# More products with the identity in the stops of TensorE, and the last rows stored by halves, in a gated linear attention with a squared-ReLU layer

## The chip, the core and the metric

The kernel runs on one NeuronCore of a Trainium2 chip. The metric is the time of one execution on the device, in microseconds; smaller is better. The core has five engines that run side by side, each with its own queue of instructions: TensorE (PE, with PEld for its weight loads), VectorE (DVE), ScalarE (ACT), GpSimd (POOL) and SyncE (SP, which here only issues transfers). They wait for one another through semaphores.

## The reference

Two stages follow each other. The first is a linear attention with a complex decay at each position, for 4 batches of 8 heads, 768 positions and 48 features; the second a layer with 2048 hidden features on the 3072 rows of 384 that come out.

```python
mag = np.sqrt(a_re * a_re + a_im * a_im)
scale = np.minimum(mag, 0.999) / (mag + 1e-06)
a_re_n, a_im_n = (a_re * scale, a_im * scale)
for t in range(S):
    ar, ai = (a_re_n[:, :, t, :, None], a_im_n[:, :, t, :, None])
    new_re = ar * S_re - ai * S_im
    new_im = ar * S_im + ai * S_re
    kv = np.einsum('bhd,bhe->bhde', k[:, :, t], v[:, :, t])
    S_re, S_im = (new_re + kv, new_im)
    y[:, :, t] = np.einsum('bhd,bhde->bhe', q[:, :, t], S_re)
...
h = x @ w_in
r = np.maximum(h, 0.0)
g = r * r
return (g @ w_out).astype(np.float32)
```

## The kernel before

The 3072 rows are cut into six units of 512 positions (`NU` = 6, `L` = 512). For each unit three things are done.

- The chain (`chain`): VectorE and ScalarE normalise the decays and multiply them up over the positions. On its way it needs four sets of three transposes on TensorE (`turned`, L1039): two of the totals (`totals`, with the matrix `perm`) and two back (`back`, with the identity). ScalarE copies their results (L1054 for the totals into `e`, L1220 for the way back into `xn`), and VectorE goes on from there. In the end it multiplies the decays into q and k (`apply`, L1259 to L1273, tile `f`).
- The pairs of heads (`pairs`): queries and keys are turned (for the first units on TensorE, L1375, copied by ScalarE into `QT` at L1379), scores are formed (L1393, tile `sc`) and masked by VectorE (L1396, tile `A`), states are summed (L1421 from the tile `KC`, which transfers bring by L1314; VectorE adds them at L1430 and L1432), and the output of the pair is made in the bank `yp` (L1445, L1449), copied by ScalarE (L1455) and carried by transfers into `xT` (L1463).
- The dense layer (`dense`), twice for each unit, 256 rows at a time (`grp`): 96 matmuls with the first weights (L1485), ReLU and square on ScalarE, and the second weights. For the first unit this is done directly (L1531). Later units use a scheme with seven products of half size in place of eight (`seven`; `half` is the product at L1582, `put`, `copy` and `add` at L1597, L1601 and L1606 are the sums around it). It fills two tiles `ot` of 128 rows by 384 columns: `o0` and `o1`. `rows` stores such a tile when it is complete, by GpSimd's queue, and for the last half of the last unit by SP's. A tile is written by halves of 192 columns, and its key in the planner is `("ot", o, c)` with the half c.

While the first unit's chain runs, the weights are read and converted on VectorE and ScalarE (`convert`, L823 to L836) as well, so VectorE has much to do before the first dense layer.

All of this is written down as steps for a planner (`Plan`). A step has an engine, an estimated duration, what it reads and writes, and a rank. `Plan.order` plays the steps through with these estimates, picks on each engine the lowest rank among those that are ready, and so fixes the order in which the instructions are emitted. The estimates matter for the order alone: on the chip the engines wait for semaphores.

In the same pass the planner looks at TensorE's stops: the time by the plan between the end of its last step and the start of the next (`stop`). Where a stop is longer than `FILL` and one of the banks d0, d1, d2 is free, it puts products of the identity with itself into that bank (L729), which nobody reads. `EACH` is the time that it reckons for one. They are emitted ahead of the step that ends the stop, so they stand in TensorE's queue before it. Each is a matmul of 128 by 128 by 128 in float32, which the trace shows as two records.

At the end VectorE has written a flag that tells whether the values allow this path; every engine loads it, branches around the general path (L1749), and the program ends when all transfers have landed (SP waits for them).

Of the kernel before, what the change touches and what calls it, by code (L numbers as in the profile page):

```python
# [480 lines left out]
class Plan:  # L481
# [4 lines left out]
    SLACK = 2.0  # L486
    RATE = 280e3
    STOP, COLD = 2.5, 3.4
    FILL, EACH = 0.8, 0.22

    def __init__(self, idle, banks):
        self.idle = idle
# [38 lines left out]
    def order(self):  # L531
        steps = self.steps
        users = [[] for _ in steps]
        left = []
        for n, s in enumerate(steps):
            left.append(len(s[2]))
            for d in s[2]:
                users[d].append(n)
        engines = {s[0] for s in steps}
        free = {e: 0.0 for e in engines}  # L540
        wait = {e: [] for e in engines}
        done, start, at = {}, {}, {}
        bus, warm = 0.0, 6.0
        self.fill = {}

        def ready(n):
            e = steps[n][0]
            t = 0.0
            for d in steps[n][2]:
                same = steps[d][0] == e and steps[d][5] is None  # L550
                hop = 0.0 if same else self.HOP[steps[d][0]]
                if e == "PE" and not same and done[d] > 100.0:
                    paired = steps[d][5] is not None and steps[n][6]
                    hop += self.SLACK if paired else self.MARGIN
                t = max(t, done[d] + hop)
            at[n] = t
            wait[e].append(n)

        for n in range(len(steps)):
            if not left[n]:  # L560
                ready(n)
        for _ in steps:
            best = None
            for e in engines:
                if not wait[e]:
                    continue
                t = max(free[e], min(at[n] for n in wait[e]))
                if best is None or t < best[0]:
                    best = (t, e)
            t, e = best  # L570
            n = min((n for n in wait[e] if at[n] <= t), key=lambda n: (steps[n][4], n))
            wait[e].remove(n)
            _, dur, _, _, _, wire, _ = steps[n]
            start[n] = t
            if e == "PE":

                stop = t - free[e]
                spare = [b for b in self.lives if self.spare(b, done, free[e])]
                if spare and stop > self.FILL:
                    self.fill[n] = int((stop - 0.3) / self.EACH), spare[0]  # L580
                elif stop > self.STOP:
                    warm = t + self.COLD
                if t < warm:
                    dur += min(dur, 0.5 * (warm - t))
            free[e] = t + dur
            if wire is None:
                done[n] = t + dur
            else:
                lat, size = wire
                bus = max(bus, t + dur) + size / self.RATE  # L590
                done[n] = max(bus, t + dur) + lat
            for m in users[n]:
                left[m] -= 1
                if not left[m]:
                    ready(m)
        self.start, self.done = start, done
        return sorted(start, key=lambda n: (start[n], n))
# [18 lines left out]
def fast_path(ctx, tc, q, k, v, a_re, a_im, moe_w_in, moe_w_out, out, flag):  # L616
# [6 lines left out]
    C = 128  # L623
    W = 4
    L = W * C
    NU = B * S // L
# [17 lines left out]
    dve, pool, act, sp = nc.vector, nc.gpsimd, nc.scalar, nc.sync  # L644
# [6 lines left out]
    def sb(name, n, dtype=F32, rows=C):  # L651
        return const.tile([rows, n], dtype, name=name)
# [8 lines left out]
    DH = DM // 2  # L661
# [20 lines left out]
    ots = [sb(f"ot{s}", DM) for s in range(NO)]  # L682
# [9 lines left out]
                                                           r=2, b=2)  # L692
# [8 lines left out]
            for n in ("d0", "d1", "d2", "sc0", "sc1", "tr0", "tr1", "yp")}  # L701
# [8 lines left out]
                     in_=turn_.rearrange("p (k x w) -> p k x w", w=4, x=4))  # L710
    pool.memset(mask, 1.0)
    for c in range(W):
        rows = mask[32 * c:32 * c + 32]
        pool.affine_select(out=rows.rearrange("p (c t) -> p c t", c=W),
                           in_=rows.rearrange("p (c t) -> p c t", c=W),
# [4 lines left out]
    for t in txs:  # L720
# [9 lines left out]
                                    stop=True), ["d2", "d1", "d0"])  # L730
# [4 lines left out]
    def tt(n):  # L735
        return n / 960.0 + 0.07
# [9 lines left out]
    def step(*args, **kw):  # L746
        return plan.add(*args, **kw)
# [4 lines left out]
    def dma(q, reads, writes, fn, rank, size, lat=1.8, group=None):  # L752
        name, dur = ("POOL", 0.55) if q is pool else ("SP" if q is sp else "ACT", 0.6)
        step(name, dur, reads, writes, fn, rank, (lat, size), group)

    CHAIN, PAIR, DENSE, CONV, LATE = 2, 1, 3, 3, 5
# [566 lines left out]
    def take(kind, n):  # L1323
        s = slot[kind]
        slot[kind] = s + 1
        if kind == "d":
            plan.lives["d%d" % (s % n)].append([])
        return s % n
# [208 lines left out]
                out=ots[o], in_=ps), (0, n))  # L1537
            rows(n, grp, i, o)

    def rows(n, grp, i, o):  # L1540
        r = n * L + (2 * grp + i) * C
        queue = sp if n == NU - 1 and grp == 1 else pool
        dma(queue, [("ot", o, 0), ("ot", o, 1)], [], lambda: queue.dma_start(  # L1543
            out=out[r:r + C, :], in_=ots[o]), (DENSE, n), C * DM * 4)

# [10 lines left out]
    def parts_of(h, up):  # L1556
        return [("w2", NT // FP * up + 2 * h + i) for i in range(2)]
# [20 lines left out]
    def half(n, b, r, h, w, wkeys, first=True, last=True):  # L1578

        def go():  # L1580
            for j in range(4 * h, 4 * h + 4):
                pe.matmul(bank[b][:, 0:DH], lhsT=g4[:, r, j], rhs=w(j),  # L1582
                          start=first and j == 0, stop=last and j == NT - 1)
        step("PE", 1.32, gk(r, h) + wkeys, [(b,)], go, (DENSE, n))

    def w_lo(c):
        return lambda j: w2[:, j, ts(c, DH)]

    def w_up(c):
        return lambda j: w2[:, NT + j, ts(c, DH)]  # L1590

    def w_t(r):
        return lambda j: TW[:, r, j]

    def put(n, o, x0, x1, op, h):
        sl = slice(4 * h, 4 * h + 4)
        step("DVE", tt(4 * C), gk(x0, h) + gk(x1, h), gk(o, h), lambda: dve.tensor_tensor(  # L1597
            out=g4[:, o, sl], in0=g4[:, x0, sl], in1=g4[:, x1, sl], op=op), (0, n))

    def copy(n, o, c, b):  # L1600
        step("ACT", ac(DH), [(b,)], [("ot", o, c)], lambda: act.copy(  # L1601
            out=ots[o][:, ts(c, DH)], in_=bank[b][:, 0:DH]), (0, n))

    def add(n, o, c, c0, b, o0=None):
        o0 = o if o0 is None else o0
        step("DVE", tt(DH) + 0.01, [("ot", o0, c0), (b,)], [("ot", o, c)], lambda: dve.tensor_tensor(  # L1606
            out=ots[o][:, ts(c, DH)], in0=ots[o0][:, ts(c0, DH)], in1=bank[b][:, 0:DH],
            op=ALU.add), (0, n))
# [19 lines left out]
    def seven(n, grp):  # L1628
        b0, b1, b2 = ["d%d" % take("d", 3) for _ in range(3)]
        o0, o1 = take("ot", NO), take("ot", NO)  # L1630
        g00, g10, g01, g11 = range(4)
        for h in range(2):
            half(n, b0, g00, h, w_lo(0), parts_of(h, 0))
            half(n, b1, g01, h, w_up(0), parts_of(h, 1))
            put(n, g10, g10, g11, ALU.add, h)
            put(n, g00, g10, g00, ALU.subtract, h)
            put(n, g01, g01, g00, ALU.subtract, h)
        copy(n, o1, 1, b0)
        add(n, o0, 0, 1, b1, o1)
        for h in range(2):  # L1640
            half(n, b2, g00, h, w_t(1), [("T", 1, h)])
            put(n, g00, g11, g00, ALU.subtract, h)
        for h in range(2):
            half(n, b0, g10, h, w_lo(1), parts_of(h, 0))
        add(n, o0, 1, 1, b2, o1)
        for h in range(2):
            half(n, b1, g00, h, w_t(0), [("T", 0, h)])
        for h in range(2):
            half(n, b2, g01, h, w_up(1), parts_of(h, 1))
        add(n, o1, 0, 1, b1, o0)  # L1650
        add(n, o1, 1, 0, b0)
        add(n, o0, 1, 1, b0)
        for h in range(2):
            half(n, b1, g11, h, w_t(2), [("T", 2, h)])
        add(n, o0, 1, 1, b2)
        rows(n, grp, 0, o0)
        add(n, o1, 0, 0, b1)
        rows(n, grp, 1, o1)

    def verdict():  # L1660
# [120 lines left out]
```

## Time and profile before

| | us |
|---|---|
| three timed executions | 703.12, 705.86, 706.57 |
| their median | 705.86 |
| the profiled execution, as the device timed it | 707.76 |
| its span, from the first to the last instruction | 705.9 |
| idle products (L729), 520 records, TensorE busy with them | 61.1 |
| L1485, first weights, 1056 records | 236.3 |
| L1582, second weights by halves, 1152 records | 199.6 |
| row stores (L1543), GpSimd and SP | 22 and 2 |

A profile is of one execution, and its times count from the start of the span. Busy time is not time on the path: idle products are busy time of TensorE, though nothing waits for what they write. A row of the order of time gives the start, the duration, the engine, the line, what is written and read, and in brackets how long the engine stood idle before it and what ended that. The mean duration of a matmul record (281 ns for an idle product) overlaps with the next; two starts tell the cost of one. The idle products stand in five places: 284 records from 1.52 us, 118 from 36.05, 8 from 49.56, 106 from 51.29 and 4 from 96.50.

### The profile page before, as it was taken

Reading aid. Unit: us, or ns where it says so; the run is one execution under the profiler, and the core shown is the slowest. Engines: PE = TensorE matmul, PEld = TensorE weight load, DVE = VectorE, ACT = ScalarE, POOL = GpSimd, SP = SyncE. Lnnn points to the kernel's source line nnn. Section 1 sums busy time; section 2 is a strip of 40 time slices with the busy share of each in tenths; the row PEclk is TensorE's granted clock in tenths of the full one; section 3 lists DMA queues with packets and bytes.
Section 4 is the critical chain, followed back from the end, with each engine's and each line's share of the span. In section 5 each row is a group of like instructions: output and inputs, shape, how many; then the busy total and the mean of one; then the engine's idle time right before and its main releaser. Section 6 shows DMA issues by size and latency. Waiting matters only on the chain.

```text
span 705.9 us, 12514 instructions
## 1 busy us (share of the span) xinstructions
PE 685.8 (97%) x4562; PEld 622.3 (88%) x4562; DVE 571.9 (81%) x1173; ACT 348.2 (49%) x578; POOL 175.7 (25%) x334
## 2 busy tenths in 40 slices
PE   9998989999999999999999999999999999999995
PEld 9998878767778999998999998988989989989995
DVE  5989899999888789997998598997699998337631
ACT  6693469955575434377424557233657242132230
POOL 6502553052400004205044050033230033032100
PEclk9999899999999999999999999999999999999998
DMA  9741459130630004735037570036550035288600
GB/s 280 218 175 27 107 134 303 60 67 22 184 88 23 1 23 119 201 86 136 11 103 189 116 154 12 1 101 178 130 153 1 24 89 132 65 294 271 202 3 26
DMA packets 56359, 79.58 MB, mean 113 GB/s; under 512 B 10944, under 2 KB 38464, under 8 KB 56288
## 3 DMA queue, kind: packets, MB, share of 16 engines
q0 software_dynamic: 15232, 40.72, 19.1%
q1 hardware_dynamic: 36928, 32.98, 18.4%
q10 hardware_dynamic: 4128, 4.98, 2.7%
q8 instruction: 38, 0.62, 0.4%
q14 instruction: 33, 0.27, 0.1%
HBM read 48.76 MB, written 4.72 MB: 76 GB/s over the span
## 4 chain that ended last, share of the span: by engine, by line
PE 66%; DVE 22%; DMA 3%; issue 3%; ACT 3%; SPq 1%; POOL 0%; DVEq 0%; ACTq 0%
PE d L1485 26%; PE d L1582 22%; PE sc L1393 4%; PE d L1531 3%; DVE f L1273 3%; DVE f L1259 2%; PE yp L1445 2%; PE tr L1421 2%; PE yp L1449 2%; DMA aq<-in_a_im_dram 2%; PE tr L1485 1%; DVE aq L1263 1%; PE sc L1485 1%; DVE f L985 1%; DVE aq L970 1%
## 5 line engine op out<-in xcount | busy, mean ns | idle before, releaser
L1485 PE MATMUL d<-xT,w 128*128 128x256 f32 x1056 | 236.3, 380 | 2.9 <-issue 2.4
L1485 PEld LDWEIGHTS d<-xT,w 128*128 128x128 f32 x1056 | 198.6, 190 | 31.9 <-issue 3.3
L1582 PE MATMUL d<-w,g 128*128 128x192 f32 x768 | 132.8, 327 | 0.1
L1582 PEld LDWEIGHTS d<-w,g 128*128 128x128 f32 x768 | 124.9, 190 | 1.7 <-issue 0.9
L1516 ACT ACTIVATE g<-d 128x512 f32<-128x512 f32 x88 | 52.1, 592 | 120.2 <-PE d L1485 87.4
L1314 POOL DMA_DIRECT2D KC<-f x160 | 78.4, 498 | 111.7 <-issue 56.4
L1543 POOL DMA_DIRECT2D out_dram<-ot x22 | 12.6, 572 | 242.2 <-DVE ot L1606 117.7
L1582 PE MATMUL d<-T,g 128*128 128x192 f32 x384 | 66.8, 327 | 0.7 <-DVE g L1597 0.7
L1582 PEld LDWEIGHTS d<-T,g 128*128 128x128 f32 x384 | 62.8, 190 | 1.4 <-DVE g L1597 1.2
L729 PE MATMUL d<-ident 128*128 128x128 f32 x520 | 61.1, 281 | 1.5 <-POOL ident masks.py:199 1.5
L903 POOL DMA_DIRECT2D v<-in_v_dram x80 | 46.4, 587 | 65.0 <-issue 32.7
L1597 DVE TENSOR_TENSOR g<-g 128x512 f32<-128x512 f32 x64 | 43.1, 684 | 23.5 <-ACT g L1517 16.4
L1517 ACT ACTIVATE g<-g 128x512 f32<-128x512 f32 x96 | 60.6, 631 | 3.0
L729 PEld LDWEIGHTS d<-ident 128*128 128x128 f32 x520 | 60.5, 197 | 1.5 <-POOL ident masks.py:199 1.5
L1393 PE MATMUL sc<-QT 96*128 96x128 f32 x368 | 48.1, 285 | 1.2 <-ACT QT L1379 1.2
L1455 ACT COPY yt<-yp 112x512 f32<-112x512 f32 x24 | 26.2, 1091 | 45.0 <-PE yp L1449 45.0
L1393 PEld LDWEIGHTS sc<-QT 96*128 96x128 f32 x368 | 45.0, 198 | 3.2 <-ACT QT L1379 1.6
L1259 DVE TENSOR_TENSOR f<-aq,xn 128x384 f32<-128x384 f32 (+1 forms) x64 | 45.1, 750 | 2.0 <-ACT xn L1220 1.9
L1273 DVE TENSOR_TENSOR f<-aq 128x384 f32<-128x384 f32 (+1 forms) x64 | 44.9, 753 | 0.6
L1531 PE MATMUL d<-w,g 128*128 128x384 f32 x128 | 44.3, 488 | 0.0
L1396 DVE TENSOR_TENSOR A<-sc,mask 128x512 f32<-128x512 f32 x45 | 29.7, 681 | 15.9 <-PE sc L1393 15.8
L985 DVE TENSOR_TENSOR f<-aq 128x384 f32<-128x384 f32 x72 | 36.9, 554 | 0.9
(195 smaller groups left out, 993.0 us busy)
## 6 DMA issues: line engine op xcount, KB each, us to landing
QT<-aq SPq DMA_DIRECT2D x128, 64.0 KB, 2.2
f<-in_moe_w_in_dram POOLq DMA_DIRECT2D x8, 768.0 KB, 7.1
f<-in_moe_w_out_dram POOLq DMA_DIRECT2D x8, 768.0 KB, 6.2
KC<-f POOLq DMA_DIRECT2D x104, 48.0 KB, 2.6
out_dram<-ot POOLq DMA_DIRECT2D x22, 192.0 KB, 2.5
QT<-aq ACTq DMA_DIRECT2D x64, 64.0 KB, 2.5
v<-in_v_dram POOLq DMA_DIRECT2D x80, 48.0 KB, 2.9
xT<-yt SPq DMA_DIRECT2D x36, 96.0 KB, 2.4
```

What stands on the lines that cost most here:

```text
L729: plan = Plan(lambda b: pe.matmul(bank[b][:, 0:C], lhsT=ident, rhs=ident, start=True, stop=True), ["d2", "d1", "d0"])
L903: lambda i=i, c=c, src=src: pool.dma_start(out=t[32 * c:32 * c + 32, i], in_=src[c]), vrank, 32 * 1536, 4.0,
L985: dve.tensor_tensor(out=f, in0=a[:, :, :, c - 1], in1=a[:, j, :, c].unsqueeze(1).to_broadcast([C, 2, HH, D]), op=ALU.mult)
L1259: lambda j=j, r=r: dve.tensor_tensor(out=f4[:, j, r], in0=a[:, r], in1=over(j), op=ALU.mult), late[z])
L1273: lambda j=j, r=r, o=o: dve.tensor_tensor(out=o[:, :, :, r * D:(r + 1) * D], in0=qk[:, j], in1=a[:, r], op=ALU.mult), late[z])
L1314: lambda i=i, c=c, queue=queue: queue.dma_start(out=kc[32 * c:32 * c + 32, i], in_=nat[32 * i:32 * i + 32, c]),
L1393: pe.matmul(sa[:, j], lhsT=T[:, j, 1, h], rhs=T[:, j, 0, h], start=True, stop=True)
L1485: pe.matmul(ps, lhsT=w1[:, f // FP, m, ts(f % FP, C)], rhs=xT[:, n % 2, m, ts(grp, G)], start=(m == 0), stop=(m == NM - 1))
L1516: act.activation(out=o, in_=ps, func=AF.Relu)
L1517: act.activation(out=o, in_=o, func=AF.Square)
L1531: pe.matmul(ps, lhsT=gt[:, f % 2, ts(i, C)], rhs=w2[:, f], start=(f == 0), stop=(f == NF - 1))
L1582: pe.matmul(bank[b][:, 0:DH], lhsT=g4[:, r, j], rhs=w(j), start=first and j == 0, stop=last and j == NT - 1)
```

## The change

A stop now gets products from 0.45 us by the plan on instead of 0.8. The number is worked out from the stop less 0.1 us instead of less 0.3, and in stops of over 5 us from 0.8 us more. The last two tiles of rows are stored by halves of their columns: `rows` is called with a half right behind the `add` that completes it, and the calls without a half do nothing for these tiles; for all other tiles it is the other way round. Four transfers of 128 rows by 768 bytes take the place of two of 128 by 1536.

```diff
-    FILL, EACH = 0.8, 0.22
+    FILL, EACH = 0.45, 0.22
...
                 if spare and stop > self.FILL:
-                    self.fill[n] = int((stop - 0.3) / self.EACH), spare[0]
+                    self.fill[n] = int((stop - 0.1 + 0.8 * (stop > 5.0)) / self.EACH), spare[0]
...
-    def rows(n, grp, i, o):
+    def rows(n, grp, i, o, half=None):
+
         r = n * L + (2 * grp + i) * C
-        queue = sp if n == NU - 1 and grp == 1 else pool
+        final = n == NU - 1 and grp == 1
+        if final and half is None:
+            return
+        queue = sp if final else pool
+        if final:
+            sl = ts(half, DH)
+            dma(queue, [("ot", o, half)], [], lambda: queue.dma_start(
+                out=out[r:r + C, sl], in_=ots[o][:, sl]), (DENSE, n), C * DH * 4)
+            return
+        if half is not None:
+            return
         dma(queue, [("ot", o, 0), ("ot", o, 1)], [], lambda: queue.dma_start(
             out=out[r:r + C, :], in_=ots[o]), (DENSE, n), C * DM * 4)
...
         add(n, o0, 0, 1, b1, o1)
+        rows(n, grp, 0, o0, 0)
...
         add(n, o1, 1, 0, b0)
+        rows(n, grp, 1, o1, 1)
         add(n, o0, 1, 1, b0)
...
         add(n, o0, 1, 1, b2)
+        rows(n, grp, 0, o0, 1)
         rows(n, grp, 0, o0)
         add(n, o1, 0, 0, b1)
+        rows(n, grp, 1, o1, 0)
         rows(n, grp, 1, o1)
```

## The prediction

> **What bounds the kernel now.** I read the page first, then the table by stretches with its granted clock, then the order of time around every place where the change adds products, and last the end of the program. The page:
>
> ```profile
> span 705.9 us, 12514 instructions
> ...
> PE 685.8 (97%) x4562; PEld 622.3 (88%) x4562; DVE 571.9 (81%) x1173; ACT 348.2 (49%) x578; POOL 175.7 (25%) x334
> ...
> PEclk9999899999999999999999999999999999999998
> ...
> PE 66%; DVE 22%; DMA 3%; issue 3%; ACT 3%; SPq 1%; POOL 0%; DVEq 0%; ACTq 0%
> ```
>
> TensorE is full, but 97% includes the idle products. The clock row has one dip, in the slice at 71 to 88 us (the one at the end is after the last matmul). The stretches around it (length, then busy time with the number of instructions for each engine, the granted clock, DMA share, GB/s):
>
> ```profile
> 5.88:74.14 68.26, 65.86 (x602) 64.78 (x600) 62.36 (x142) 45.24 (x72) 26.68 (x45) 1.00 0.54 169
> 74.14:77.55 3.41, 1.82 (x17) 1.57 (x16) 3.20 (x9) 1.28 (x2) 0.34 (x1) 1.00 0.23 57
> 77.55:84.38 6.83, 6.75 (x34) 6.27 (x36) 5.65 (x12) 1.50 (x4) 3.57 (x8) 0.50 0.71 169
> ...
> 103.10:105.40 2.30, 0.00 (x0) 0.00 (x0) 2.27 (x3) 1.28 (x2) 2.30 (x5) 1.00 0.81 193
> 105.40:702.00 596.60, 588.35 (x3710) 529.08 (x3710) 480.72 (x981) 284.11 (x481) 130.87 (x241) 1.00 0.39 106
> ```
>
> So there are two regimes. From 105.4 us TensorE works without stops, and a delay ahead of it moves the end one for one. Before that VectorE sets the pace, and TensorE's products with the identity only fill its stops. For 6.83 us TensorE ran at half clock, straight after 3.41 us in which it was busy for 1.82.
>
> The order of time where the products are added (start, duration, operation, idle time before it and what ended that):
>
> ```profile
> 32.83 0.51 ACT L1000 COPY xn<-aq 128x384 f32<-128x384 f32 x1 [4.58 <-DVE aq L993]
> ...
> 35.40 0.82 PE L1039 MATMUL tr<-perm,xn 128*128 128x128 f32 x6
> 35.92 0.48 ACT L1054 COPY e<-tr 128x384 f32<-128x384 f32 x1 [1.39 <-PE tr L1039]
> ...
> 36.05 13.34 PE L729 MATMUL d<-ident 128*128 128x128 f32 x118
> ...
> 36.45 0.35 DVE L1013 TENSOR_TENSOR f<-f 128x192 f32<-128x192 f32 x1 [0.79 <-DVE f L1013]
> ...
> 54.40 0.84 ACT L1220 COPY xn<-tr 128x384 f32<-128x384 f32 x2
> ...
> 64.55 1.95 PE L1375 MATMUL d<-ident,f 128*96 128x128 f32 x16 [1.26 <-DVE f L1273]
> ...
> 77.63 3.79 PE L1393 MATMUL sc<-QT 96*128 96x128 f32 x16 [0.37 <-ACT QT L1379]
> ...
> 79.75 0.69 DVE L1396 TENSOR_TENSOR A<-sc,mask 128x512 f32<-128x512 f32 x1 [0.59 <-PE sc L1393]
> ...
> 81.46 0.69 DVE L1396 TENSOR_TENSOR A<-sc,mask 128x512 f32<-128x512 f32 x1 [0.55 <-PE sc L1393]
> ...
> 87.45 0.25 DVE L1430 COPY St<-tr 96x96 f32<-96x96 f32 x1 [0.84 <-PE tr L1421]
> ...
> 88.03 1.95 PE L1393 MATMUL sc<-QT 96*128 96x128 f32 x16
> ```
>
> The first long stop is overfilled already: xn was there at 33.34, the transposes that read it began at 35.40, right behind the last idle product, and VectorE stood 0.79 us behind ScalarE's copy of their result. The 16 score records at 77.63 took twice what the same 16 take at 88.03.
>
> **What the Trainium skill says.** "TensorE: Matmul & The Clock Gate", Part 1 (the HAM clock gate): TensorE drops to half clock after a window of about 3.4 us with too little work, and the windows run freely, whatever the kernel does. The trace agrees on the length (6.83 us is two windows of 3.41) and on the half. It differs on "idle": 1.82 us of 3.41 were busy and it dropped all the same. "DMA: Bandwidth & Descriptors", Anatomy of one DMA, puts some 2 us of fixed cost on each transfer, whatever its size; here the row stores take a median of 2.5 us to land.
>
> **The change, part by part.** The planned orders of the two programs differ on TensorE only in the idle products: 142 become 146 ahead of the transposes at 35.40, 59 become 64 ahead of those at 49.23, 4 become 5 ahead of 50.93, 53 become 58 ahead of 64.55, 2 new ones come ahead of the scores at 77.63, and 2 become 3 ahead of the products at 97.11. That is 18 more. No other engine's order moves, but for SP's stores at the end. One product is two records; 59 of them run from 36.05 to 49.23, so one costs 0.223 us.
>
> First stop: 4 x 0.223 = 0.89 us later. VectorE already stands there waiting for what follows, so all of it goes onto its chain: +0.89. Bounds: 0.4, if the clock is granted earlier in another execution and the stop is less overfilled, to 0.89.
>
> Second and third: transposes at 49.23 + 0.89 + 5 x 0.223 = 51.24, and the next at about 52.7 instead of 50.93. What reads them is ScalarE's copy at 54.40, which moves to 55.29 with VectorE. Cost nothing; the cover is over 2 us.
>
> Fourth: its products start 1.72 later and are 5 more, so they end at 51.29 + 1.72 + 58 x 0.223 = 65.94, when f has been ready since 64.55 + 0.89 = 65.44. TensorE is 0.5 us late against VectorE. The mask at 69.35 came some 1.0 us after the scores that it reads were done (half of 67.32 to 69.2), so it doesn't wait; the stops of 0.82 and 0.47 us for the KC transfers at 75.0 and 76.0 swallow the rest. Nothing; up to 0.5 if that cover is thinner.
>
> The two new ones: the pause is 0.37 us and they take 0.45, so +0.08. They raise the busy time of the weak window from 1.82 to 2.27 us, and the 0.5 us lateness closes part of the pauses before. If that keeps the full clock, the scores take 1.79 instead of 3.58 us and the three transposes at 81.21 1.41 instead of 2.70: 3.08 us on TensorE. What VectorE gains is only what it stood waiting: 0.59 + 0.55 + 0.84 = 1.98. The third part also needs the KC transfers of the second half, issued by SP to 83.98 at 0.63 us each, so I take 1.9 (bounds: 1.1 without the third wait, 3.08 if TensorE itself sets the pace up to 99). VectorE being the pace up to 105, this goes to the end.
>
> The last: 3 x 0.223 = 0.67 from 96.50 ends at 97.17, and the products behind wait for VectorE's mask of 96.56 to 97.24 anyway. Nothing.
>
> The stores: the four halves are issued by SP behind the add that completes each. The last one still waits for the last add (698.56, 0.35) and is issued at 698.94. It carries 96 KB instead of 192. Behind it SP branches, and only then waits for landings:
>
> ```profile
> L1749 SPq EVENT_SEMAPHORE  x8: 17/17/17, 702.3 to 702.8; - x8
> ...
> L1749 POOLq COMPARE_BRANCH  x1: 54/54/54, 675.7 to 675.7; - x1
> ...
> L1749 SPq COMPARE_BRANCH  x1: 50/50/50, 699.3 to 699.3; - x1
> ```
>
> From SP's branch to its next instruction are 2.9 us, so the store, which lands within about that, is hidden behind the branch. GpSimd's same branch at 675.7, with no store near it, took 2.6 us to its next instruction (678.3). So at most some 0.4 us of SP's branch can be blamed on the store's traffic, and half the bytes should give back most of it: -0.3 (bounds 0 and -0.45; above 0 only if two more issues of 0.35 us delayed the last one, and the halves before it are issued 2 us and more earlier).
>
> Sum: +0.89 + 0.08 - 1.9 - 0.3 = -1.2 us on the span of 705.9, that is 704.7. The profiled execution took 707.76 us around that span, 1.9 above the median of 705.86; the same difference from that median gives 704.6.
>
> **Rivals.**
>
> The half clock moves instead of going. Nothing fills the stop at 103.1 to 105.4, in which TensorE has no work at all. In the profile a window edge (77.55 + 8 x 3.413 = 104.86) cut it in two. With work arriving 1.2 us earlier it lies at 101.9 to 104.2, inside one window, which then holds about 1.1 us of work, less than the 1.82 that was not enough. Then 6.83 us at half clock fall where TensorE is the bound: +3.4, and the sum is +2.2: 708.1, slower. It decides as soon as a window holds the whole pause; against it: the windows are not tied to the kernel, so it strikes a part of the executions only, and may have struck timed ones of the kernel before too.
>
> No clock is gained: the two products are too few, or the timed executions mostly don't have the dip. Then +0.97 - 0.3 = +0.7: 706.5. For it: the three times spread from 703.12 to 706.57, about one dip, so one of them may be without. Against it: two of three lie high.
>
> More is gained: TensorE's whole 3.08 us, or a second dip that timed executions had at 105 and now miss (3.4). With the store -2.5 to -4.7: 703.4 to 701.2. For it the spread again, against it that the profile shows one dip and VectorE full.
>
> **How the numbers follow.** Forecast 0.42 (704.6, itself 703.4 to 705.6 by the bounds), dip moved 0.22 (708.1), nothing gained 0.18 (706.5), more gained 0.18 (701.2 to 703.4). A half per cent is 3.5 us, about what a measurement can tell from no change: under 702.3 is faster, over 709.4 slower. Faster: the better part of the last case and a tail of the first, 0.2. Slower: a tail of the moved dip with the first stop's full delay, 0.09. The same 0.71. The range leaves out the ends of the last case and of the moved dip: 702.0 to 708.3.
>
> **What would show it.** In the changed profile: the transposes of the first stop about 0.9 us later and VectorE's wait there at 1.6 to 1.7 us; full clock from 77 to 85, scores in under 2 us, no VectorE wait on sc; SP's next instruction 2.5 to 2.7 us behind its branch. Wrong would be a half clock in 104 to 112 (first rival), one still at 78 (second), or VectorE waiting at its masks near 69 because the fourth stop's extra products had no cover.

## The result and the profile after

The changed kernel took 706.44 us, the median of 22 executions; the kernel before, on the same chip, took 705.06 (22 executions). One of the 22 of the changed kernel took 1048 us at a mean granted clock of 0.643 and stays out of the ratio. The ratio is 1.002, 95% interval 1.0011 to 1.003: slower by some 1.4 us (0.8 to 2.1) where 1.2 us less had been forecast. The profiled execution took 706.87 us around a span of 705.1; that of before had 707.76 and 705.9. So the two profiles stand the other way round from the medians, and what follows reads places in them, not their totals.

The page of the kernel after:

```profile
span 705.1 us, 12590 instructions
...
PE 687.4 (97%) x4598; PEld 625.3 (89%) x4598; DVE 572.1 (81%) x1173; ACT 347.8 (49%) x578; POOL 176.7 (25%) x334
...
PEclk9999999999999999999999999999999999999999
```

TensorE has 36 records more, the 18 added products. The dip that the clock row showed at 71 to 88 us is gone from the row, but a slice is 17.6 us long. The table by stretches, cut where the granted clock changes and at steps of 3.41 us from there, shows what the row hides (length, then busy time and instructions of each engine, granted clock, DMA share, GB/s):

```profile
74.08:77.50 3.42, 2.79 (x36) 2.39 (x32) 3.35 (x8) 1.09 (x1) 0.28 (x1) 1.00 0.19 47
77.50:84.32 6.82, 6.55 (x69) 5.87 (x68) 6.58 (x17) 3.21 (x5) 3.91 (x8) 1.00 0.80 180
84.32:87.74 3.42, 1.85 (x18) 1.69 (x19) 2.58 (x7) 1.90 (x4) 2.25 (x5) 1.00 0.30 76
87.74:91.15 3.41, 3.41 (x19) 3.39 (x17) 2.68 (x4) 2.17 (x3) 1.67 (x4) 0.50 0.31 73
```

The stretch of 77.5 to 84.3 us, at half clock before, now has the full one. Behind it is a new weak window, 84.32 to 87.74, with 1.85 us of work, and the half clock follows it, for one window in place of two. The order of time tells where the work of 84 to 92 us went (start, duration, engine, line, and in brackets the idle time before it and what ended that):

```profile
78.26 2.05 PE L1393 MATMUL sc<-QT 96*128 96x128 f32 x16
...
84.48 0.51 PE L1421 MATMUL tr<-v,KC 128*96 128x48 f32 x4 [0.43 <-DMA KC<-f]
...
85.27 0.85 PE L1421 MATMUL tr<-v,KC 128*96 128x48 f32 x8 [0.28 <-DMA KC<-f]
...
87.25 0.51 PE L1421 MATMUL tr<-v,KC 128*96 128x48 f32 x4 [1.13 <-DMA KC<-f]
...
87.80 0.25 DVE L1432 TENSOR_TENSOR S<-tr,St 96x96 f32<-96x96 f32 x1 [0.81 <-PE tr L1421]
...
88.32 3.31 PE L1393 MATMUL sc<-QT 96*128 96x128 f32 x16
...
90.27 0.69 DVE L1396 TENSOR_TENSOR A<-sc,mask 128x512 f32<-128x512 f32 x1 [0.49 <-PE sc L1393]
...
91.66 0.69 DVE L1396 TENSOR_TENSOR A<-sc,mask 128x512 f32<-128x512 f32 x1 [0.70 <-PE sc L1393]
```

The scores at 78.26 run at full speed and VectorE waits for none of them. TensorE, no longer slowed, is through with the first half sooner than the transfers of the next one into `KC`: it stands 0.43, 0.28 and 1.13 us for them, and these pauses make the weak window. In this execution the price comes back: VectorE waits 0.81 us for the products behind these pauses and 0.49 and 0.70 us for the scores at half clock, where in the profile before it waited 0.59 and 0.55 for the scores ahead and 0.84 for the state's products. Against the profile before, VectorE is 0.86 us late at 77.1 us (times of before), 1.30 us early at 87.5 and 0.77 us late again at 90.9.

The first stop:

```profile
32.09 0.51 ACT L1000 COPY xn<-aq 128x384 f32<-128x384 f32 x1 [4.58 <-DVE aq L993]
...
36.27 0.82 PE L1039 MATMUL tr<-perm,xn 128*128 128x128 f32 x6
36.79 0.48 ACT L1054 COPY e<-tr 128x384 f32<-128x384 f32 x1 [3.00 <-PE tr L1039]
...
37.31 0.35 DVE L1013 TENSOR_TENSOR f<-f 128x192 f32<-128x192 f32 x1 [2.40 <-issue]
```

The transposes begin 0.87 us later than before (36.27 against 35.40), and VectorE stands idle for 2.40 us in place of 0.79. Of the 1.61 us more, only 0.87 is the change's. In this execution VectorE and ScalarE had come to `xn` 0.74 us sooner (32.09 against 32.83), and the stop took that lead away too, because its length is fixed by a number of products and not by the arrival of `xn`.

At the end of the program the waits of SP's queue show its branch (line that waited, what it waited for, us in total, times, the longest), here before, after, and in e2, one of the experiments below, which has the stores of the kernel before:

```profile
SPq L1749 <- SPq L1749: 2.9, 1, 2.9
...
SPq L1764 <- SPq L1764: 2.5, 1, 2.5
...
SPq L1751 <- SPq L1751: 2.6, 1, 2.6
```

From the branch to SP's next instruction are 2.5 us in place of 2.9, as the prediction had it from half the bytes. But the stores don't explain it: with the stores of before, the profiles of e2, e4, e6, e7 and e10 show 2.6 us and those of e5, e8 and e11 2.8; with the stores by halves, e1, e3 and e9 show 2.6 to 2.7.

### The profile page after: what moved, and what is told of

Read it like the earlier page. It is cut to its first block, busy times and chain, and to the rows that moved or that the text cites. A ratio compares the mean times of both kernels' runs of the same rounds, so it can differ in the third digit from the quotient of the medians.

```text
span 705.1 us, 12590 instructions
## 1 busy us (share of the span) xinstructions
PE 687.4 (97%) x4598; PEld 625.3 (89%) x4598; DVE 572.1 (81%) x1173; ACT 347.8 (49%) x578; POOL 176.7 (25%) x334
## 3 DMA queue, kind: packets, MB, share of 16 engines
q10 hardware_dynamic: 4128, 4.98, 2.7%
## 4 chain that ended last, share of the span: by engine, by line
PE 61%; DVE 26%; DMA 4%; issue 3%; ACT 2%; SPq 1%; POOL 0%; ACTq 0%; DVEq 0%
PE d L1485 23%; PE d L1593 21%; PE sc L1393 4%; DVE f L1259 4%; DVE f L1273 3%; PE d L1531 3%; PE tr L1421 2%; PE yp L1445 2%; DMA aq<-in_a_im_dram 2%; DVE aq L1263 2%; PE yp L1449 2%; PE tr L1485 2%; PE sc L1485 1%; DMA KC<-f 1%; DVE f L985 1%
## 5 line engine op out<-in xcount | busy, mean ns | idle before, releaser
L729 PE MATMUL d<-ident 128*128 128x128 f32 x556 | 65.3, 281 | 1.5 <-POOL ident masks.py:199 1.5
L729 PEld LDWEIGHTS d<-ident 128*128 128x128 f32 x556 | 64.6, 197 | 1.5 <-POOL ident masks.py:199 1.5
```

The source lines that it names most:

```text
L729: plan = Plan(lambda b: pe.matmul(bank[b][:, 0:C], lhsT=ident, rhs=ident, start=True, stop=True), ["d2", "d1", "d0"])
```

## The experiments

All act as the kernel before with one or two edits, except two that say otherwise. A table `COUNT` sets how many idle products are emitted ahead of a step: 110 is the first stop's transposes, 142, 145 and 218 are the second to fourth stop, 246 is the scores at 77.6 us, 359 the last stop. These are the edits with the counts of the kernel before (not shown is the changed line with the stop less 0.1 us, which all these kernels have too):

```diff
-    FILL, EACH = 0.8, 0.22
+    FILL, EACH = 0.45, 0.22
+    COUNT = {110: 142, 142: 59, 145: 4, 218: 53, 246: 0, 359: 2}
...
             many, b = self.fill.get(n, (0, None))
+            many = self.COUNT.get(n, many)
```

So the change's rule decides only where products may stand, and `COUNT` how many do. The profiles agree: e2 has 528 records of idle products, 8 more than before for its four products. Further down only the line of `COUNT` is shown. In these kernels' profiles the line numbers are two higher than in the kernel they start from (L1041 are the transposes). Each was timed beside the kernel before, e5 to e8 on another chip than the rest and e11 on a third: 22 executions each, but 14 of e4, e5 and e6, 6 of e7, 8 of e8 and 16 of e11. The ratio is to the kernel before on the same chip, and a change in microseconds worked out from it uses 705.5.

| run | edit | median, us | median before | ratio, 95% interval |
|---|---|---|---|---|
| e1_stores | stores by halves alone | 705.41 | 705.5 | 1.0005, 0.9995 to 1.0015 |
| e2_first146 | first stop 146 alone | 706.57 | 705.5 | 1.0024, 1.0013 to 1.0035 |
| e3_all_but_first | the whole change, first stop 142 | 706.04 | 705.5 | 1.001, 1.0001 to 1.0019 |
| e4_first132 | first stop 132 alone | 704.02 | 705.5 | 0.9984, 0.997 to 0.9997 |
| e5_pause2 | two products in the pause alone | 705.0 | 705.7 | 0.9995, 0.9983 to 1.0006 |
| e6_stops_2to4 | stops two to four alone | 705.56 | 705.7 | 1.0, 0.999 to 1.0009 |
| e7_first162 | first stop 162 | 710.37 | 705.7 | 1.0077, 1.0058 to 1.0096 |
| e8_132_pause2 | first stop 132, pause 2 | 703.56 | 705.7 | 0.9963, 0.9948 to 0.9978 |
| e9_after132 | the whole change, first stop 132 | 704.32 | 705.56 | 0.9989, 0.998 to 0.9998 |
| e10_first122 | first stop 122 | 703.39 | 705.56 | 0.9974, 0.9964 to 0.9983 |
| e11_122_pause2 | first stop 122, pause 2 | 703.79 | 704.8 | 0.9982, 0.9972 to 0.9992 |

**One part alone: the stores (e1_stores).** The `rows` part of the change, with the counts of before. The new calls, beside the changed `rows`:

```diff
+    COUNT = {110: 142, 142: 59, 145: 4, 218: 53, 246: 0, 359: 2}
...
+        rows(n, grp, 0, o0, 0)
...
+        rows(n, grp, 1, o1, 1)
...
+        rows(n, grp, 0, o0, 1)
...
+        rows(n, grp, 1, o1, 0)
```

> The kernel before with the stores by halves alone; all idle products as before. Theory (the four products in the first long stop make the loss, the stores give a little back): 0.4 us faster than before, from SP's branch, which takes 2.5 instead of 2.9 us to its next instruction. Rival (the two more transfers on SP cost time at the end): 0.5 us slower or more.

Nothing that the timing can tell: between -0.4 and +1.1 us. SP's branch is 2.6 us in this profile, but so it is in five profiles without this edit, so it says nothing about the stores.

**One part alone: the first stop (e2_first146).**

```diff
+    COUNT = {110: 146, 142: 59, 145: 4, 218: 53, 246: 0, 359: 2}
```

> The kernel before with 146 instead of 142 products in the first long stop, nothing else. Theory: 0.9 us slower, since VectorE already waits there. Rival (VectorE waits there in the profiled execution only, and the loss comes from the longer fourth stop): within 0.3 us of before.

+0.24%, that is +1.7 us (0.9 to 2.5). The first stop alone makes the kernel as slow as the whole change does. The sign is the theory's and its 0.9 is the interval's lower end; whether more than that is chance is not settled. In its profile VectorE waits at the stop for 1.66 us.

**All but the first stop (e3_all_but_first).** The changed kernel with 142 products there.

```diff
+    COUNT = {110: 142, 142: 64, 145: 5, 218: 58, 246: 2, 359: 3}
```

> The whole change, but with 142 products in the first long stop. Theory: the changed kernel less 0.9 us, so 0 to 0.5 us slower than before. Rival (the longer fourth stop makes the loss): still 1.4 us slower.

+0.7 us (0.1 to 1.3), between the theory's 0 to 0.5 and the rival's 1.4: the rest of the change, with its clock gain and its stores, gains nothing and seems to cost a little.

**The opposite: a shorter first stop (e4_first132).**

```diff
+    COUNT = {110: 132, 142: 59, 145: 4, 218: 53, 246: 0, 359: 2}
```

> The kernel before with 132 products in the first long stop, ten fewer. Theory: they were too many already in the kernel before; TensorE is free 2.2 us earlier, VectorE's wait of 0.8 us there goes, and the kernel is 0.8 to 1.5 us faster than before. Rival (the stop is not on the path): no change. Half the clock lost at the start of the next work: slower.

-1.1 us (-2.1 to -0.2), within what was expected. In its order of time the stop is no longer overfilled: TensorE itself waits for `xn`, and VectorE no longer waits. Not all of the gain need come from that: as the granted clocks will show (e5), this kernel also lost the half clock at 77 us in most executions.

```profile
32.74 0.51 ACT L1002 COPY xn<-aq 128x384 f32<-128x384 f32 x1 [4.54 <-DVE aq L995]
33.31 0.53 PEld L1041 LDWEIGHTS tr<-perm,xn 128*128 128x128 f32 x5 [0.57 <-ACT xn L1002]
33.31 0.77 PE L1041 MATMUL tr<-perm,xn 128*128 128x128 f32 x5 [0.33 <-ACT xn L1002]
...
35.71 0.36 DVE L1015 TENSOR_TENSOR f<-f 128x192 f32<-128x192 f32 x1
```

**The pause alone (e5_pause2).** The two products that were to keep the clock, without the rest.

```diff
+    COUNT = {110: 142, 142: 59, 145: 4, 218: 53, 246: 2, 359: 2}
```

> The kernel before with one edit: two idle products in the short pause ahead of the scores at 77.6 us; every other stop and the stores as before. Theory (the two products take away a half clock that most executions of the kernel before have, and the rest of the change gives that back): -0.5 to -1.2 us against before (the trace of the first-stop run put the half clock's price on VectorE's chain at about 2.1 us, but it isn't in every execution); in its profile no half clock at 77 to 84, scores in under 2 us. Rival (the half clock only moves on, to the pauses at 84 to 88 or at 103 to 105, whenever it leaves this place): -0.2 to +0.5 us, and a half clock at one of these places in its profile.

-0.4 us (-1.2 to +0.4). The profile has full clock from 6.82 us to the end, and the scores at 77.32 take 2.05 us; the mechanism worked and the time hardly moved. Each timed execution is listed with its mean granted clock, and these say why. In the thirteen profiled executions this mean is 0.992 to 0.994 where the half clock lasted two windows, 0.995 or 0.996 where it lasted one, and 0.997 to 0.999 where there was none before the last matmul. At 0.994 or less, so with about the long dip, were 102 of the 160 executions of the kernel before that were timed beside e1 to e11, and none of the 14 of this one. But in the four groups of before's executions, these were on average only 1.3, 1.1, 1.0 and 0.7 us longer than the others. So an estimate of what could be won on the mean is 102/160 x 1.1 = 0.7 us, where the prediction had credited 1.9.

**The later stops alone (e6_stops_2to4).**

```diff
+    COUNT = {110: 142, 142: 64, 145: 5, 218: 58, 246: 0, 359: 2}
```

> The kernel before with one edit: 64, 5 and 58 idle products in the second, third and fourth stop in place of 59, 4 and 53; the first stop, the pause and the stores as before. Theory of the prediction (these stops have cover): 0, within 0.3 us of before, and no wait of VectorE at its masks near 69 us. Rival (TensorE's later arrival behind the fourth stop is handed on to the copies and masks of 65 to 85 us, or to the second half's transfers, and is what keeps the change without the first stop's products from gaining): +0.5 to +1.0 us, with VectorE over 0.4 us behind the kernel before at 87 us.

0 (-0.7 to +0.6), as the theory had it; VectorE doesn't wait at its masks near 69 us, and at 87 us it is 2.7 us ahead of the profile before, not behind as the rival had it. Two of 14 executions were at 0.994 or less in clock, against 20 of 29 of the kernel before: closing the pauses at 73 to 77 us took the dip away as well, without the two products. At the price above that alone should have gained some 0.6 us. That the time didn't move leaves room for a cost of as much elsewhere, which the interval hides and no wait in the profile shows.

**Five times the dose (e7_first162).**

```diff
+    COUNT = {110: 162, 142: 59, 145: 4, 218: 53, 246: 0, 359: 2}
```

> The kernel before with one edit: 162 idle products in the first long stop in place of 142. Theory (the stop is overfilled at 142, and each product more delays the end by its own 0.22 us): +4.5 us by the product's price, +3.8 to +4.8 with what the moved half clock gives or takes. Rival (VectorE catches up in the later stops, so that the first four cost little and the rest of the loss is elsewhere): under +3 us.

The medians differ by 4.7 us, the ratio gives 5.4 (4.1 to 6.8), for 20 x 0.223 = 4.5, with 6 executions only: each product more goes to the end in full. The order of time at the stop:

```profile
31.99 0.51 ACT L1002 COPY xn<-aq 128x384 f32<-128x384 f32 x1 [4.55 <-DVE aq L995]
...
40.04 0.82 PE L1041 MATMUL tr<-perm,xn 128*128 128x128 f32 x6
...
41.09 0.35 DVE L1015 TENSOR_TENSOR f<-f 128x192 f32<-128x192 f32 x1 [6.26 <-issue]
```

VectorE had come 0.84 us sooner than in the profile before and stands 6.26 us. At 77 us it is still 4.63 us late, so none of this is made up in the later stops.

**The two together (e8_132_pause2).**

```diff
+    COUNT = {110: 132, 142: 59, 145: 4, 218: 53, 246: 2, 359: 2}
```

> The kernel before with two edits: 132 idle products in the first long stop in place of 142, and two in the short pause ahead of the scores at 77.6 us. Theory (the first stop costs what it overfills, the pause gains by the clock, and both add): -1.6 to -2.4 us, the shorter first stop's -1.1 us and the pause's -0.5 to -1.2 together. Rival (an earlier start only shifts which window is weak, and the clock is lost at another place): no better than the shorter first stop alone, -1.1 us or less.

-2.6 us (-3.7 to -1.5) by the ratio, with few executions (8), 2.1 by the medians: both effects' size, as the theory had it. The profile is that of the slowest of the eight, one of three at 0.994 or less in clock, and it shows the rival's mechanism: the half clock is there, two windows from 75.59 us, ahead of where the two products are emitted. The weak window has moved forward with the work.

```profile
72.18:75.59 3.41, 1.96 (x23) 1.55 (x20) 3.31 (x9) 1.68 (x2) 0.06 (x1) 1.00 0.24 49
75.59:82.42 6.83, 6.83 (x34) 6.73 (x34) 4.96 (x12) 0.58 (x1) 3.90 (x8) 0.50 0.78 177
```

**The changed kernel with a shorter first stop (e9_after132).**

```diff
+    COUNT = {110: 132, 142: 64, 145: 5, 218: 58, 246: 2, 359: 3}
```

> The changed kernel with one edit: 132 idle products in the first long stop in place of 146; all else of the change is kept. Theory (the overfilled first stop decides the changed kernel; the rest of the change is worth about nothing): 704.0 to 704.6 us, that is -1.0 to -1.6 us against the kernel before, and about -2.2 us against the changed kernel. Rival (the extra products of the later stops cost the change about a microsecond, as the whole change without the first stop's four measured 0.7 us above before): -0.5 us or less gained against before, 705 us or more.

704.32, inside the theory's 704.0 to 704.6: faster than before by 0.8 us (0.1 to 1.4) by the ratio, a little less than the theory's 1.0, and by 1.2 by the medians. One number, 132 in place of 146, turns the change's sign, and takes some 2.2 us off it (from +1.4 to -0.8).

**Shorter still (e10_first122).**

```diff
+    COUNT = {110: 122, 142: 59, 145: 4, 218: 53, 246: 0, 359: 2}
```

> The kernel before with one edit: 122 idle products in the first long stop in place of 142. Theory (with 132 VectorE no longer waits at this stop, so that ten products less free nothing more): the same as with 132, -0.8 to -1.6 us against before, and TensorE standing 1 to 2 us idle ahead of the transposes. Rival (the stop is still overfilled in many executions at 132, or the stop left open costs the clock): -2 us or more for the first; 0 or above before, with a half clock within 10 us of this stop, for the second.

-1.8 us (-2.5 to -1.2), at the far end of what the theory expected and between it and the first rival; the intervals of 132 and 122 overlap. The profile at the stop:

```profile
32.12 0.51 ACT L1002 COPY xn<-aq 128x384 f32<-128x384 f32 x1 [4.55 <-DVE aq L995]
32.68 0.53 PEld L1041 LDWEIGHTS tr<-perm,xn 128*128 128x128 f32 x5 [1.98 <-ACT xn L1002]
32.68 0.77 PE L1041 MATMUL tr<-perm,xn 128*128 128x128 f32 x5 [1.75 <-ACT xn L1002]
```

In this execution `xn` came early, at 32.12, as it did after the change; with 122 the transposes follow at once and VectorE keeps its lead. With 132 and an `xn` as early (32.14 in e8) the products stood in the way: the transposes began at 33.86. But VectorE had other work until then and didn't wait; the `f` that it makes from them starts at 35.20 in both. So this stop doesn't show what the ten products less would gain. TensorE's 1.75 us of idle time cost no clock near the stop. The clock explains a part: at 0.994 or less were 1 of these 22 executions and 2 of the 14 of e4, against 29 of 43 and 42 of 67 of the kernel before. At the 1.0 and 1.3 us that such executions were longer there, some 0.6 us of either gain would be the half clock's, and the rest the stop's; these are estimates, and no run separates the two.

**Both, from 122 (e11_122_pause2).**

```diff
+    COUNT = {110: 122, 142: 59, 145: 4, 218: 53, 246: 2, 359: 2}
```

> The kernel before with two edits: 122 idle products in the first long stop in place of 142, and two in the short pause ahead of the scores. Theory (the first stop gains what it was overfilled by, the pause what half clock is left; both are small and add): -2.0 to -2.8 us against before, 702.8 to 703.6. Rival (with 122 few executions have a half clock there any more, so the pause has nothing left to gain): -1.4 to -2.0 us, as 122 alone.

-1.3 us (-2.0 to -0.6): no more than 122 alone, as the rival had it. With 122 one of 22 executions was at 0.994 or less in clock, with 122 and the pause none of 16, so there was no half clock of two windows left for the pause to remove. The four kernels with a shorter stop and none of the change's other parts but the pause are all faster than before and than the changed kernel; their order among themselves isn't settled.

## Why the prediction was wrong

- First stop, +0.89: right in the trace (+0.87), and e2 and e7, with more products there, show that it is on the path. In the time it is +1.7 (0.9 to 2.5), at least what was predicted. Its lower bound of 0.4 wasn't needed. In the five profiles with 142 products the transposes do begin earlier when the full clock does: at 34.77 us with the full clock from 4.56 (e3), 34.97 from 4.98 (e6), 35.10 from 5.25 (e1), 35.40 from 5.88 (before) and 35.85 from 6.82 (e5). But `xn` came earlier in the other four as well, and VectorE waits 0.60 to 1.42 us in all five.
- Second, third and fourth stop, nothing: e6 gives 0, though together with the loss of the dip, so a hidden cost is not excluded. In the changed profile ScalarE's copy went from 54.40 to 55.27, moved by VectorE alone, and the mask of 70.22 has no wait.
- Two products before the scores, to keep the clock there: they ran (0.68 us as recorded), and the stretch behind has full clock. The account by which they do it was partly wrong. They stand at 77.73, just behind the window of 74.08 to 77.50, so they didn't fill it; it rose from 1.82 to 2.79 us of recorded work because the later arrival closed the pauses in it, which the prediction had named only as a second help. e6, without the two, shows the same.
- **The half clock gone, -1.9: the step that failed, as a term that was sized too large.** On VectorE's chain it is right: in the ten profiles without the half clock at 77 us, VectorE gains 2.1 to 2.3 us on the profile before between 77 and 88 us. But the term took one profiled execution for all, though 58 of 160 executions of before had no such dip to lose. And it took the gain to go to the end one for one, though over whole executions the dip goes with 0.7 to 1.3 us. Together that is some 0.7 us on the mean; measured alone the term is -0.4 (-1.2 to +0.4). The prediction's own rival had said that an execution may be without the dip, but the sum didn't weigh it.
- What came next in the changed profile: the prediction looked for the next late thing only at the pause at 103 us. In this profile it was the transfers into `KC`, which its own text named as needed for its third wait: TensorE came earlier, they came no earlier (SP issued its eight from 79.67 to 84.69, up to 83.98 before), and 1.84 us of stops and a half clock at 87.74 took VectorE's gain back by 91 us. The other nine profiles keep their gain to 91 us. And the nine executions of the changed kernel at 0.995 or 0.996 in clock took 706.42 us on average, the twelve at 0.997 or more 706.41. So among these executions a short half clock shows no cost in time.
- Last stop, nothing: nothing in the runs contradicts it; it wasn't tried alone.
- The stores, -0.3: the time did not become shorter (1.0005). The term was read from a difference of two branches in one execution; SP's branch takes 2.6 to 2.8 us in eight other profiles with the old stores, so 2.9 was the upper end of a spread.
- The sum with measured terms: +1.7 for the first stop, 0 for the later stops, -0.4 for the pause, +0.4 for the stores gives +1.7, and +1.4 was measured; with the intervals of these terms the sum is uncertain by about 1.5 us.

Of the rivals, "no clock is gained" gave the nearest time, 706.5, but by luck: the clock was gained (none of 21 executions at 0.994 or less), and it was the gain in time that stayed small. "The half clock moves" was right about the mechanism in the changed profile, but it named 104 to 112 us and a full loss of 3.4 us. That place did show in e7, where the half clock lay from 105.23 to 108.65. The forecast had the cost on the chain right and lost its direction by setting a sure 0.89 against an unsure 1.9.

What stays open: 0.89 for the first stop less 0.7 for the clock is +0.2, and some 1.2 us of the measured +1.4 are traced to no wait. e2 measured more than four products' worth. And e3, with 3 of 22 executions at 0.994 or less, should have gained some 0.6 us and lost 0.7: compared within the three groups of clock it is 0.9 us (0.4 to 1.4) above the kernel before. That is a comparison of executions that sorted themselves, not an experiment, and e3's profile shows VectorE 3.0 us ahead at 104 us, so the loss lies later, if it is one. The prediction's reading that from 105.4 us on a delay goes to the end one for one holds only on the mean: between 104 us and its last instruction VectorE gains 1.5 us on the profile before in e1 and loses 2.0 in e2. They part at stops near 390 to 410 and 490 to 513 us; one, at 390 us in e2, ends with a transfer into `QT`, and the others were not followed to their cause. So no single profile's end can be used to judge a change this small.

## What to carry to other kernels

Filler work with a fixed count delays whatever stands behind it in its queue as soon as the awaited data comes early: check in several executions whether the consumer waits behind the last filler, and take products away until it doesn't. A gain that is read from a state which comes and goes (here the granted clock) has to be weighed by how many executions are in it and by what whole executions lose to it, and a certain cost of half its size can outweigh it. Before a difference between two profiles is put down to the change, look at the same place in a profile that doesn't have it, as here with SP's branch. When an engine is sped up, look at once for what it will then wait for in the very next stage.

## What the runs showed of the hardware

The half clock doesn't follow TensorE's recorded busy time alone. "TensorE: Matmul & The Clock Gate", Part 1 (the HAM clock gate) of the Trainium skill gives half clock after at least one idle window of about 3.4 us. Here windows with 1.82 us (before), 1.85 (after) and 1.96 us (e8) of recorded work were followed by it, which differs from "idle"; and one with less kept the full clock. The stretches of e6_stops_2to4 and of e1_stores:

```profile
97.14:100.55 3.41, 1.59 (x8) 1.44 (x8) 3.31 (x5) 3.41 (x6) 3.41 (x7) 1.00 0.68 159
100.55:103.97 3.42, 2.63 (x13) 2.03 (x12) 3.39 (x4) 1.19 (x2) 3.42 (x7) 1.00 0.98 202
```

```profile
73.52:76.93 3.41, 2.01 (x21) 1.79 (x20) 3.27 (x9) 1.59 (x2) 0.05 (x1) 1.00 0.32 81
76.93:83.76 6.83, 6.83 (x34) 6.35 (x36) 6.03 (x13) 1.67 (x3) 3.87 (x8) 0.50 0.70 155
```

1.59 us in 8 records kept it, 2.01 us in 21 records lost it. The 21 are matmuls with 48 or 128 columns, the 8 are of the dense layer, with 256 columns, so a record's length may overstate how much a small matmul counts. What does sort the windows is the number of columns that pass through, the last number of the right operand in a row of the order of time, added up over the records that start in the window. The six windows that the half clock followed have 768 to 1392 columns, and the other 2598 at full clock in the thirteen profiles, from the start of the full clock to 690 us, 1536 or more. A window at half clock was followed by another one where it had 1920 or 1936 columns, and by the full clock where it had 2048 or more. This is a count from traces after the fact; no run set the columns to test it.

The drop lasted two windows in before, e1 and e8 and one in after, e3 and e7. And where the windows lie against the kernel is different in every execution: the full clock began between 4.36 and 7.33 us from the start of the span in the profiles of this case.
